# A planned attention and FFN kernel on one core: Sinkhorn of batch 0 ahead, a written-out order, and the last two output projections by Strassen blocks

## The chip, the cores and the metric

The kernel runs on one core of one Trainium2 chip. TensorE multiplies matrices into PSUM, VectorE (DVE), ScalarE (ACT) and GpSimd (POOL) work on what it leaves, and SyncE (SP) and GpSimd issue the transfers between the DRAM and the on-chip SBUF. The metric is the device time of one execution in microseconds (us); less is better. A profiled execution leaves a trace, and a profile page is made from it.

## What is computed

Inputs are q, k and v of shape (4, 8, 768, 64): 4 batches, 8 heads, 768 tokens, 64 wide; `sort_net` (4, 8, 8, 8); and three weight matrices.

```python
P = sort_net                                   # (4, 8, 8, 8)
for _ in range(5):                             # Sinkhorn
    P = exp(P - max(P, axis=-1))
    P = P / (sum(P, axis=-1) + 1e-9)
    P = P / (sum(P, axis=-2) + 1e-9)
k_sorted = einsum('bhij,bhjcd->bhicd', P, k in 8 blocks of 96)
v_sorted = einsum('bhij,bhjcd->bhicd', P, v in 8 blocks of 96)
attn = softmax(q_block @ k_sorted_block.T / 8)  # each block of 96 tokens with its own block only
x = (attn @ v_sorted_block) as (3072, 512)
out = ((x @ w_a) * (x @ w_b)) @ w_out           # 512 -> 1536 -> 512
```

## The kernel before

**Pieces of work and a planner.** The kernel doesn't issue instructions as it goes. It collects pieces of work with `add(engine, duration, function, deps, get, put, rank)` (L49): the engine, or several that could do it, each with an assumed duration; the pieces it depends on; the buffers that it takes and gives back; and a rank. `Plan.solve` (L132) simulates the engines with these durations, with fixed delays between engines (L39) and with a limited number of buffers and PSUM banks. At each step it takes the piece that can start first, and among those that can start within a small margin the one of lowest rank. If a piece may run on two engines, the engine where it would end first is taken. The result, sorted by start, is the order in which `emit` (L992) issues everything; on the chip each engine then works through its own queue in that order. `_fill` (L177) puts warm-up matmuls on zeros into TensorE's planned gaps up to 32.6 us.

**Loads.** GpSimd issues all loads of q, k, v and of the weights, cast to bf16 on the way: k, v and half of q of four head pairs of batch 0, then w_a and w_b in four pieces (`load_ab`, L377) with the other halves of q between the first and the second piece, then batches 1, 2 and later 3. SP issues `sort_net`, the way of v through DRAM (`v_out`, L544; `v_back`, L548), two kinds of transposing transfers and the stores.

**Sinkhorn** (L412 to L453). The 32 matrices of all batches lie one to a partition, 32 x 64. Each of five iterations is an exponential on ScalarE and six VectorE operations, each waiting for the one before. The result is copied out 16 times (`p_rep`), turned by eight small matmuls (`spread_ops`, L432) and multiplied with a mask into `s_all` (`spread`, L439): batch 0 on VectorE, batches 1 to 3 later on GpSimd (`later_spreads`, L455). `s_all` is what k and v are mixed with.

**Attention** goes by head pair (two heads, 128 rows). `mix_half` and `mix_part` mix and transpose k and v with `s_all` on TensorE, `q_part` transposes q, `so_part` (L693) does the scores, the exponential, the product with v and the division, and `x_part` or a transposing transfer puts the result into `xT`. Batch 0 goes in two halves of four blocks each, so that its first half can go on early; later batches go whole, between the other work.

**Up projection.** Batch 0 is done plainly (`ab_plain`, L745): for each of 2 token halves and 12 tiles of the hidden width, four matmuls of 384 columns with w_a, four with w_b; ScalarE copies the first result out (L755), VectorE multiplies the two (L760) into `hT`. Batches 1 to 3 use the Winograd form of Strassen's seven products (`ab_strassen`, L810): the operands are cut into 2 x 2 blocks, seven block products take the place of eight. The sums of weight blocks are made once (`w_sums`, L769, on GpSimd, between the loads); the sums of x per batch (`x_sums`, L789). A chain of products accumulates in one PSUM bank, and between two products of it ScalarE copies out what stands there ("snap", L840); VectorE adds such copies to other banks ("plus", L848). All elementwise operations of two tensors are recorded at L306, the helper `tt`.

**Output projection** (`out_plain`, L893): for each batch, token half and chunk of 128 tokens, 12 matmuls of 512 columns (L899) of `hT` with `w_out_sb` into one bank, of which ten can go before the last tiles of h are there; ScalarE or VectorE copies the bank out, and SP stores it with two transfers (L919).

**Order of the main loop** (L962): the output of batch b, attention of b + 2, loads of b + 3, then the up projection of b + 1.

Of the kernel before, what the change touches and what calls it, by code (L numbers as in the profile page):

```python
# [21 lines left out]
class Op:  # L22
# [3 lines left out]
                 "left", "users", "seq", "ready")  # L26

    def __init__(self, alts, fn, deps, get, put, rank, lat, seq):
        self.alts, self.fn, self.get, self.put = alts, fn, get, put
        self.deps = [d for d in deps if d is not None]  # L30
        self.rank, self.lat, self.seq = rank, lat, seq
        self.start = self.end = self.eng = None
        self.users, self.left, self.ready = [], 0, 0.0


class Plan:
# [12 lines left out]
    def add(self, eng, dur, fn, deps=(), get=(), put=(), rank=0.0, lat=None):  # L49
        alts = dict(eng) if isinstance(eng, (list, tuple)) else {eng: dur}  # L50
        op = Op(alts, fn, deps, list(get), list(put), rank, lat, len(self.ops))
# [80 lines left out]
    def solve(self):  # L132
# [5 lines left out]
        at = dict(self.AT)  # L138
        ready = [op for op in self.ops if op.left == 0]
        done = 0  # L140
        while ready:
            cands = {}
            for op in ready:
# [4 lines left out]
                ends = {e: max(at[e], w) + d for e, d in op.alts.items()}  # L148
                e = min(ends, key=ends.get)
                cands.setdefault(e, []).append((max(at[e], w), op))  # L150
            pick = None
            for e, c in cands.items():
                lo = min(s for s, _ in c) + self.EPS[e]
                s, op = min(((s, o) for s, o in c if s <= lo), key=lambda x: (x[1].rank, x[1].seq))
# [5 lines left out]
            s, e, op = pick  # L160
            ready.remove(op)
            op.start, op.eng, op.end = s, e, s + op.alts[e]
            at[e] = op.end
            self._take(op, s)
# [27 lines left out]
STRASSEN_AB = (1, 2, 3)  # L192
STRASSEN_OUT = ()
# [5 lines left out]
def kernel(  # L199
# [86 lines left out]
    ring("o", 3, [P, DMODEL], FP32)  # L286
# [7 lines left out]
    p_col = const.tile([P, NB, BH], BF16, name="p_col")  # L294
    p_nat = const.tile([BH, NB, NB], FP32, name="p_nat")
    ident = const.tile([P, P], BF16, name="ident")
    mask = const.tile([P, CG], BF16, name="mask")
    rsum = const.tile([BH, NB], FP32, name="rsum")
    csum = const.tile([BH, NB], FP32, name="csum")
    p_fin = const.tile([BH, NB, NB], BF16, name="p_fin")  # L300
    p_rep = const.tile([BH, NB, NB, CG], BF16, name="p_rep")
    warm_sb = const.tile([P, 512], BF16, name="warm_sb")
# [15 lines left out]
    def sp_dma(issue, work, fn, deps, get=(), put=(), rank=0.0):  # L318
        i = add("SP", issue, fn, deps, get=get, rank=rank, lat=0.6)
        return add("DQ", work, None, [i], put=put, rank=rank - 100.0, lat=1.5)  # L320

    o_p = add("SP", 0.1, lambda: nc.sync.dma_start(
        out=p_nat, in_=sort_net.rearrange("b h i j -> (b h) i j")), lat=1.5)
# [739 lines left out]
```

The softmax here doesn't subtract the row's maximum and nothing guards it: scores larger than these inputs give would overflow.

## Time and profile before

| | us |
|---|---|
| median of three runs | 245.91 (245.87 to 340.56) |
| profiled execution | 245.06 |
| its span, first to last instruction | 243.3 |
| TensorE (PE) busy | 233.7 |
| VectorE (DVE) busy | 150.1 |
| ScalarE (ACT) busy | 125.3 |
| GpSimd (POOL) busy, with its issuing of loads | 119.6 |
| output projection, 288 matmuls of 512 columns | 66.4 |
| up projection of batch 0, 192 matmuls of 384 columns | 39.2 |
| warm-up matmuls of 512 columns, 38 | 10.8 |

The granted TensorE clock is 1.0 throughout. A row of a timeline has start, duration, engine, line, operation, what is written and read, and in brackets how long the engine was idle before and what ended that. A row of the chain has start, duration, engine, tensor and line, and "issue" is time in which the engine waited for nothing that the profile shows. A row of a window has its bounds and length, and then the busy time of TensorE, of its weight loads, of VectorE, ScalarE and GpSimd, the clock, the share of the DMA engines and GB/s. A matmul's listed duration overlaps its neighbour's, so the pace of a run of matmuls is its time divided by their number.

### The profile page before, as it was taken

Reading aid. Unit: us, or ns where it says so; the run is one execution under the profiler, and the core shown is the slowest. Engines: PE = TensorE matmul, PEld = TensorE weight load, DVE = VectorE, ACT = ScalarE, POOL = GpSimd, SP = SyncE. Lnnn points to the kernel's source line nnn. Section 1 sums busy time; section 2 is a strip of 40 time slices with the busy share of each in tenths; the row PEclk is TensorE's granted clock in tenths of the full one; section 3 lists DMA queues with packets and bytes.
Section 4 is the critical chain, followed back from the end, with each engine's and each line's share of the span. In section 5 each row is a group of like instructions: output and inputs, shape, how many; then the busy total and the mean of one; then the engine's idle time right before and its main releaser. Section 6 shows DMA issues by size and latency. Waiting matters only on the chain.

```text
span 243.3 us, 5723 instructions
## 1 busy us (share of the span) xinstructions
PE 233.7 (96%) x2204; PEld 132.4 (54%) x2204; DVE 150.1 (62%) x348; ACT 125.3 (52%) x243; POOL 119.6 (49%) x132
## 2 busy tenths in 40 slices
PE   6998999999989999999999999999999999999992
PEld 2466766666655554665544455665654455565440
DVE  6656654654555738589987452988862448886210
ACT  3366646468655533667654443766631076673100
POOL 8979999999970020069755110173540007355000
PEclk9999999999999999999999999999999999999999
DMA  5999999999965683619998867200035450000135
GB/s 67 180 203 187 202 203 187 167 191 178 162 134 107 167 184 78 149 16 154 135 175 110 192 174 178 46 0 0 3 66 108 96 122 0 1 0 3 43 86 129
DMA packets 50106, 27.90 MB, mean 115 GB/s; under 512 B 28832, under 2 KB 47008, under 8 KB 50080
## 3 DMA queue, kind: packets, MB, share of 16 engines
q0 software_dynamic: 24112, 14.16, 43.3%
q1 hardware_dynamic: 25968, 13.38, 25.7%
q8 instruction: 17, 0.28, 0.5%
q14 instruction: 9, 0.07, 0.1%
HBM read 30.29 MB, written 8.26 MB: 158 GB/s over the span
## 4 chain that ended last, share of the span: by engine, by line
PE 67%; ACT 1%; DVE 1%; issue 0%; ACTq 0%; DVEq 0%
PE ps L831 33%; PE ps L899 26%; PE ps L593 2%; PE ps L578 2%; PE ps L489 1%; PE ps L537 1%; PE ps L473 1%; PE ps L749 1%; ACT f L840 0%; DVE xp L604 0%; ACT o L248 0%; DVE a L306 0%; DVE rec L599 0%; ACTq L840 0%; DVEq L306 0%
## 5 line engine op out<-in xcount | busy, mean ns | idle before, releaser
L306 POOL TENSOR_TENSOR hT<-a,f 128x384 bf16<-128x384 bf16 x39 | 35.5, 918 | 78.1 <-DVE f L306 56.3
L899 PE MATMUL ps<-w_out_sb,hT 128*128 128x512 bf16 x288 | 66.4, 379 | 0.0
L840 ACT COPY f<-ps 128x384 f32<-128x384 f32 x108 | 48.2, 482 | 23.6 <-PE ps L831 21.1
L899 PEld LDWEIGHTS <-hT 128*128 128x128 bf16 x288 | 27.0, 98 | 30.1
L306 DVE TENSOR_TENSOR a<-f,ps 128x384 bf16<-128x384 f32 x54 | 29.4, 549 | 10.4 <-PE ps L831 6.4
L306 DVE TENSOR_TENSOR f<-f,ps 128x384 f32<-128x384 f32 x54 | 28.9, 550 | 8.9 <-PE ps L831 6.0
L583 ACT ACTIVATE eT<-ps 96x768 bf16<-96x768 f32 x32 | 24.9, 806 | 17.2 <-PE ps L578 16.9
L306 DVE TENSOR_TENSOR hT<-a,ps 128x384 bf16<-128x384 bf16 x42 | 23.1, 551 | 12.4 <-PE ps L749 6.9
L248 ACT COPY o<-ps 128x512 f32<-128x512 f32 x15 | 8.8, 585 | 36.3 <-PE ps L899 36.3
L831 PE MATMUL ps<-tx,ws_a 128*128 128x384 bf16 x108 | 25.2, 326 | 0.2 <-ACT f L840 0.2
L831 PE MATMUL ps<-tx,ws_b 128*128 128x384 bf16 x108 | 24.9, 326 | 0.3 <-ACT f L840 0.3
L604 DVE TENSOR_TENSOR xp<-ps,rec 96x512 bf16<-96x512 f32 x32 | 21.4, 677 | 0.4
L749 PE MATMUL ps<-xT,w_a_sb 128*128 128x384 bf16 x96 | 19.6, 327 | 0.0
L749 PE MATMUL ps<-xT,w_b_sb 128*128 128x384 bf16 x96 | 19.6, 326 | 0.0
L831 PEld LDWEIGHTS <-ws_b 128*128 128x128 bf16 x144 | 13.8, 98 | 10.1 <-ACT f L840 0.9
L755 ACT CAST a<-ps 128x384 bf16<-128x384 f32 x24 | 11.5, 479 | 14.9 <-PE ps L749 9.1
L250 DVE COPY o<-ps 128x512 f32<-128x512 f32 x9 | 6.2, 691 | 20.8 <-PE ps L899 20.7
L831 PEld LDWEIGHTS <-ws_a 128*128 128x128 bf16 x144 | 13.5, 98 | 10.1 <-ACT f L840 1.4
L831 PE MATMUL ps<-xT,w_b_sb 128*128 128x384 bf16 x72 | 17.6, 326 | 0.3 <-DVE xp L604 0.2
L831 PE MATMUL ps<-xT,w_a_sb 128*128 128x384 bf16 x72 | 17.5, 326 | 0.0
L831 PEld LDWEIGHTS <-w_b_sb 128*128 128x128 bf16 x108 | 10.4, 98 | 7.9 <-DVE xp L604 0.7
L831 PEld LDWEIGHTS <-w_a_sb 128*128 128x128 bf16 x108 | 10.3, 98 | 7.9 <-ACT f L840 0.6
(90 smaller groups left out, 337.9 us busy)
## 6 DMA issues: line engine op xcount, KB each, us to landing
out_dram<-o SPq DMA_DIRECT2D x48, 128.0 KB, 2.4
k<-in_k_dram POOLq DMA_DIRECT2D x16, 192.0 KB, 6.1
v<-in_v_dram POOLq DMA_DIRECT2D x16, 192.0 KB, 6.1
vd<-vm SPq DMA_DIRECT2D x10, 192.0 KB, 2.9
vs<-vd SPq DMA_DIRECT2D x10, 192.0 KB, 3.1
q<-in_q_dram POOLq DMA_DIRECT2D x16, 96.0 KB, 6.9
w_a_sb<-in_moe_w_a_dram POOLq DMA_DIRECT2D x4, 384.0 KB, 7.1
w_b_sb<-in_moe_w_b_dram POOLq DMA_DIRECT2D x4, 384.0 KB, 9.0
```

What stands on the lines that cost most here:

```text
L248: nc.scalar.copy(out=out, in_=in_)
L250: eng.tensor_copy(out=out, in_=in_)
L306: ENG[eng].tensor_tensor(out=out, in0=in0, in1=in1, op=op)
L578: nc.tensor.matmul(sc[:, e, i * BLK:(i + 1) * BLK], lhsT=kT[e * D:(e + 1) * D, at:at + P], rhs=rhs, start=True, stop=True)
L583: nc.scalar.activation(out=buf(("eT", b, p, h))[:, :, 0:HB], in_=buf(("sc", b, p, h))[0:BLK, :, 0:HB], func=AF.Exp, scale=float(scale))
L593: nc.tensor.matmul(ops_[:, e, i * OW:(i + 1) * OW], lhsT=eT[:, e, i * BLK:i * BLK + P], rhs=vs[:, h * NBH + i, e * OW:(e + 1) * OW], start ...
L604: nc.vector.tensor_tensor(out=_ap(xp, h * NBH * 2 * D, [[NB * 2 * D, BLK], [D, 2], [2 * D, NBH], [1, D]]), in0=_ap(ops_, 2, [[1024, BLK], ...
L749: nc.tensor.matmul(pf[:, 0:HW], lhsT=w_sb[:, kc, m * P:(m + 1) * P], rhs=buf(("xT", b))[:, kc, t * HW:(t + 1) * HW], start=(kc == 0), stop ...
L755: ea = add("ACT", 0.48, lambda: nc.scalar.copy(out=buf(("a", b, t, m)), in_=buf(("pf", b, t, m, "a"))[:, 0:HW]), [pa], get=[("a", ("a", b, ...
L831: nc.tensor.matmul(buf(key)[:, 0:HW], lhsT=lf(j), rhs=rf(j), start=start and j == 0, stop=j == 1, skip_group_check=not start)
L840: return add("ACT", 0.48, lambda: nc.scalar.copy(out=buf((name, b, g, n)), in_=buf(kA)[:, 0:HW]), [dep], get=[("f", (name, b, g, n))], rank=r)
L899: nc.tensor.matmul(po, lhsT=hT[:, t * 2 + m // G, m % G, c * P:(c + 1) * P], rhs=w_out_sb[:, m, :], start=(m == 0), stop=(m == KO - 1), sk ...
```

## The change

1. **Sinkhorn.** Batch 0 gets its own, with its 64 rows (8 heads x 8 rows) on 64 partitions. Row sums come from the exponential's accumulator or VectorE's; column sums of a head come from a small f32 matmul with a constant matrix that is one within a head. It ends in one matmul and the same spread. Batches 1 to 3 run the old five iterations on 24 partitions, after batch 0's, with a later rank (12); their copies, matmuls and spreads also come later.
2. **Output projection of batches 2 and 3** by seven block products (`out_strassen`): tokens in two halves, hidden width in two halves, 256 output columns. Per batch 24 sums of `hT` blocks (VectorE or GpSimd) into buffers of k and v that are free by then; once 8 sums of `w_out` (`o_sums`) into buffers of q and kT. Per chunk of 128 tokens seven products of six matmuls of 256 columns, three ScalarE snapshots and four VectorE sums out of PSUM, and two stores of two transfers each.
3. **Planner.** A piece of work can be marked to use the SBUF port that VectorE and GpSimd share (`port`); marked pieces on these engines don't overlap in the plan. The order and, where there is a choice, the engine of every piece are no longer chosen by rank but read from a literal, `ORDER`.
4. **Smaller edits.** The weight pieces load in the order 0, 2, 1, 3. The weight sums of the second piece may run on VectorE too. One more output buffer, and four that lie in `s_all`. The warm-up matmuls read from a part of `ws_b`. The up projection of batch 3 starts after the fifth product of batch 2's last output chunk. Assumed durations: scores 0.33 for 0.23, v's way through DRAM with 3.0 for 1.5 in batch 1.

```diff
+        def begin(op, e, w):
+            return max(at[e], w, port) if e in op.port else max(at[e], w)
...
+        while ready:
+            s, e, op = given() if order else greedy()
...
+            if e in op.port:
+                port = op.end
...
-STRASSEN_OUT = ()
+ORDER = (
...
+STRASSEN_OUT = (2, 3)
+PLAIN_G = 6
...
-    for c in range(1, 4):
+    for c in (2, 1, 3):
         load_ab(c)
...
+    x = step("ACT", 0.28, lambda: nc.scalar.activation(
+        out=pa[:, 1, :], in_=pa[:, 0, :], func=AF.Exp, accum_out=ps1), [o_p0])
+    x = step("DVE", 0.15, lambda: nc.vector.reciprocal(out=pc1, in_=ps1), [x])
+    x = step("DVE", 0.21, lambda: stt(p_exp, _ap(pa, NB, [[2 * NB, HN], [0, H], [1, NB]]), pc1,
+                                      m_same), [x, o_same])
+    x = step("PE", 0.2, sk_turn, [x, o_row], get=[("bank", bank)])
+    x = step("DVE", 0.19, lambda: nc.vector.reduce_sum(
+        out=ps1, in_=buf(bank)[0:HN, 0:NB], axis=AX.X), [x])
+    x = step("DVE", 0.15, lambda: nc.vector.reciprocal(out=pc1, in_=ps1), [x])
+    for it in range(4):
+        x = step("ACT", 0.24, lambda it=it: nc.scalar.activation(
+            out=pa[:, 1, :], in_=px if it else buf(bank)[0:HN, 0:NB], func=AF.Exp, scale=pc1), [x])
+        x = step("PE", 0.2, sk_rows, [x, o_same])
+        x = step("DVE", 0.19, lambda: nc.vector.reciprocal(out=pr, in_=buf(bank)[0:HN, NB:2 * NB]),
+                 [x], put=[bank])
+        x = step("DVE", 0.25, lambda: stt(px, pa[:, 1, :], 1.0, pr, ps1), [x])
+        x = step("DVE", 0.15, lambda: nc.vector.reciprocal(out=pc1, in_=ps1), [x])
...
+    def out_strassen(b, rk, wt_ok):
...
+            todo = ((0, lambda g=g: (hb(1, 0, g), hb(1, 1, g)), ALU.add, h21 + h22, None),
+                    (1, lambda g=g: (sb(0, g), hb(0, 0, g)), ALU.subtract, h11, 0),
+                    (2, lambda g=g: (hb(0, 0, g), hb(1, 0, g)), ALU.subtract, h11 + h21, None),
+                    (3, lambda g=g: (hb(0, 1, g), sb(1, g)), ALU.subtract, h12, 1))
...
+            s1 = snap("os1", p1)
+            p2 = pe(kX, h(0, 1), wo(1, 0), True, True, hd(0, 1, first) + wo_in, rk + 0.1,
+                    get=[("bank", kX)], gs=first)
+            p2 = pe(kX, h(0, 1), wo(1, 0), False, True, hd(0, 1, late) + [p2], rk - 0.4, gs=late)
+            c11 = plus("os1", kX, 0, 0, [s1, p2], [kX, ("os1", b, c)])
+            p6 = pe(kA, s(1), wt(1), False, True, [s1] + sd(1) + td(1), rk, put=sput(1) + tput(1))
+            u2 = snap("ou2", p6)
+            p5 = pe(kY, s(0), wt(0), True, True, sd(0) + td(0), rk + 0.1, get=[("bank", kY)],
+                    put=sput(0) + tput(0))
+            st["lasty", b] = p5
+            p7 = pe(kA, s(2), wt(2), False, True, [u2] + sd(2) + td(2), rk, put=sput(2) + tput(2))
+            u3 = snap("ou3", p7)
+            p4 = pe(kZ, h(1, 1), wt(3), True, True, [p1, p2] + hd(1, 1) + td(3), rk + 0.6,
+                    get=[("bank", kZ)], put=tput(3))
+            c22 = plus("ou3", kY, 1, 1, [u3, p5], [("ou3", b, c)])
+            c21 = plus("ou3", kZ, 1, 0, [u3, p4], [kZ, ("ou3", b, c), ("och", b, c)])
+            p3 = pe(kY, s(3), wo(1, 1), False, True, [c22] + sd(3), rk, put=sput(3))
+            c12 = plus("ou2", kY, 0, 1, [u2, p3], [kY, ("ou2", b, c), ("och", b, c)])
...
     for b in range(B):
-        for t in range(2):
-            for c in range(3):
-                out_plain(b, t, c, RB + 40.0)
+        if b in STRASSEN_OUT:
+            if wt_ok is None:
+                wt_ok = o_sums(RB - 10.0)
+            out_strassen(b, RB + 40.0, wt_ok)
+        else:
+            for t in range(2):
+                for c in range(3):
+                    out_plain(b, t, c, RB + 40.0)
```

## The prediction

> **What bounds the kernel now.** I read the page first: busy shares, then the chain that ended last.
>
> ```profile
> span 243.3 us, 5723 instructions
> PE 233.7 (96%) x2204; PEld 132.4 (54%) x2204; DVE 150.1 (62%) x348; ACT 125.3 (52%) x243; POOL 119.6 (49%) x132
> ...
> PE ps L831 33%; PE ps L899 26%; PE ps L593 2%; PE ps L578 2%; PE ps L489 1%; PE ps L537 1%; PE ps L473 1%; PE ps L749 1%; ACT f L840 0%; DVE xp L604 0%; ACT o L248 0%; DVE a L306 0%; DVE rec L599 0%; ACTq L840 0%; DVEq L306 0%
> ```
>
> TensorE is busy 96% of the span, and the chain is its own queue: the up projections (L831) and the output projection (L899), one matmul after another. So only two things can save time: fewer TensorE microseconds, or fewer microseconds in which it does nothing useful. The chain in order of time shows the second half piece by piece (start, duration, what):
>
> ```profile
> 118.46 0.49 ACT f L840
> ...
> 126.05 0.04 issue
> 126.09 0.49 ACT f L840
> ...
> 151.01 0.19 issue
> 151.20 0.21 DVE rec L599
> 151.42 0.02 issue
> 151.44 0.70 DVE xp L604
> ...
> 238.68 0.02 issue
> 238.70 0.59 ACT o L248
> ```
>
> The breaks are few: 0.56 us at 118.4, 0.6 at 126.0, 1.2 at 151.0, and 1.05 more at 210.8. The last matmul ends at 238.68, and 4.6 us of eviction and store follow.
>
> The start is the other loss. In the timeline:
>
> ```profile
> 2.29 0.26 ACT L414 ACTIVATE p_nat<-p_nat 32x64 f32<-32x64 f32 x1 [0.27 <-DMA p_nat<-in_sort_net_dram]
> ...
> 13.47 0.36 PE L435 MATMUL ps<-ident,p_rep 32*128 32x32 bf16 x8
> ...
> 14.42 0.38 PE L500 MATMUL ps<-s_all,k 128*64 128x64 bf16 x12
> ```
>
> Before 14.42 TensorE has only transposes of q and warm-up matmuls on zeros (L983), which count as busy. The Sinkhorn chain from 2.29 to 13.95 sets this. From the middle of the kernel I take the windows of one stage each (columns: window, length, then busy microseconds by engine): up projection of batch 2, its output projection, up projection of batch 3, and the rest.
>
> ```profile
> 152.00:182.00 30.00, 29.83 (x193) 17.78 (x193) 24.54 (x52) 18.78 (x43) 13.64 (x15) 1.00 0.11 23
> 182.00:195.00 13.00, 13.00 (x63) 5.92 (x61) 4.45 (x8) 1.76 (x3) 0.00 (x0) 1.00 0.47 101
> 195.00:225.00 30.00, 29.90 (x181) 17.34 (x180) 22.16 (x44) 18.91 (x43) 12.73 (x14) 1.00 0.10 23
> ```
>
> TensorE is full; VectorE (third busy number) is at 82% beside an up projection and 34% beside an output projection; GpSimd (fifth) has room.
>
> **Change, part 1: Sinkhorn of batch 0 first, alone, in another layout.** Now one iteration takes 1.76 us (the exponentials start at 2.29, 4.05, 5.81, 7.57, 9.33), then replication until 12.60 (ScalarE's copy waits behind a q copy), a matmul at 13.47 held back by warm-up matmuls, the spread at 13.95. New, from the rows of small instructions: exponential 0.26, reciprocal 0.19, multiply 0.21, TensorE step about 0.2 (one small matmul takes 0.17 to 0.21), 0.12 from TensorE to VectorE (13.83 to 13.95), 0.03 to 0.04 at each other handover. First round: 0.26 + 0.19 + 0.21 + 0.2 + 0.12 + 0.21 + 0.19 + 5 x 0.035 = 1.55. Each of the four others: exponential, TensorE, reciprocal, multiply with sum (0.25), reciprocal: 0.26 + 0.2 + 0.12 + 0.19 + 0.25 + 0.19 + 4 x 0.035 = 1.35, together 5.4. Last multiply, one matmul, handover 0.6. From 2.29 this is 9.85: 4.1 us earlier than 13.95. Below: each of the six TensorE steps stands in a queue with q transposes that wait for loads and with warm-up matmuls; one such delay cost 0.87 here (12.60 to 13.47), so six eat 5.2 and the gain is nothing. Above: the 0.87 of now goes too, 4.4 at most, for what follows is set by loads. Landings (issue plus time to landing): v of pairs 0 to 3 at 7.7, 10.6, 13.1 and 15.5, w_b's first piece at 20.3. The fourth pair's v is mixed at 18.66 now, so it can move by 3.1; w_b's first use is at 28.12, so that is no limit. TensorE, ScalarE and VectorE have other mixes in the meantime. I take 3.6 us, nearer the upper end, since the four loads allow 3.1 and the chain 4.1.
>
> What moves behind: the Sinkhorn of batches 1 to 3, 5 x (0.26 + 1.27) + 0.41 x 2 + 0.42 = 9 us of small work, mostly VectorE's, now has to be done before batch 1 is mixed (48.4 now). VectorE is busy 15.3 of 24 us from 16 to 40, and 5.6 of 10 after: it fits, as long as ready evictions are not queued behind it; if that cover went, up to 9. The three spreads of 2.0 on GpSimd's queue move behind the weight loads; those issued at 17.6 and 20.4 now behind spreads can go earlier, but the transfers are at 200 GB/s from 12 us on, so they land little sooner. The second small load on SP costs one issue (0.41), hidden under the table load (to 2.02). The weight pieces in the order 0, 2, 1, 3 cost nothing: piece 1 lands at 23.7 and 25.7, and TensorE has half 1 of batch 0 until then. Eight sums of w on VectorE (0.55) instead of GpSimd (1.66) free 13 us of GpSimd, which is nobody's limit there (all sums done by 71.4, first needed at 99).
>
> **Part 2: output projection of batches 2 and 3 by seven products.** Removed: 2 x 72 matmuls of 512 columns, 144 x 0.216 (12 in 2.59) = 31.1. Added: 2 x 126 of 256 columns. No row has 256; 384 columns cost 0.1636 (154 in 25.19), so a straight line through 384 and 512 gives 0.111: 252 x 0.111 = 28.0. Gain 3.1. Ends: 0.108 (half of 512) gives 3.9; 0.1636 loses 10.1; it breaks even at 0.123. Each matmul loads its own weights, 98 ns, below 0.111, and rows of 128 columns run eight in 0.45 with weight loads between, so I stay on the line.
>
> The Trainium skill speaks against this step. TensorE: Matmul & The Clock Gate, section Back-to-back issue gap, gives a sustained pace of about 81 ns at 128 columns and 131 ns at 512 when weights are loaded each time; interpolated (an estimate from that page), 252 x 98 ns against 144 x 131 ns would be a loss of 5.8 us. The trace has 216 ns at 512 columns with a weight load each, so the measurement decides.
>
> Added beside it: per batch 24 sums of h (128x384, bf16), 9 ScalarE snapshots, 12 VectorE sums out of PSUM; once 8 sums of w_out; gone: 6 evictions a batch. Prices: a sum of h lies between half of the 768-wide bf16 row (0.55 / 2 = 0.28) and the 384-wide row with an f32 input (0.556); 0.33, nearest to the row of its own type. On GpSimd 0.92. A sum out of PSUM: between 0.55 x 256/384 = 0.37 and 0.55, 0.42. A snapshot 0.38 (0.48 at 384, 0.585 at 512), 18 of them 6.8 on ScalarE, which is at 63% and falls to 14%: hidden. VectorE from 152 to the end: 53.6 + 48 x 0.33 + 24 x 0.42 + 8 x 0.55 - 4 x 0.69 = 81.1 of about 83.6 us of TensorE time. That is too full; with 28 of the sums on GpSimd it is 71.9, or 86%. What does TensorE lose at such a load? From 110 to 130 VectorE is busy 9.08 and 8.78 of 10 us, and TensorE loses 0.25 and 0.29: 2.7%, over 83.6 us 2.3; at 82% (152 to 182) it loses 0.17 in 30. I take 1.3 us; ends 0 and, with all on VectorE and its idle 18% kept, 81.1 / 0.82 - 83.6 = 15.
>
> GpSimd and VectorE clearly meet in one place: a GpSimd sum at 139.12 begins under a VectorE sum and takes 1.83 instead of 1.63 us. So a meeting costs 0.2; fifteen of them 3 us of slack, inside the 15. The Trainium skill (SBUF — State Buffer, section SBUF: two separate sides) is harder: two-input VectorE operations and GpSimd operations exclude each other for the whole instruction. By it, as an estimate, 48 sums that meet GpSimd's share of 31% and wait half of 0.92 lose 6.8 us. No run here shows this.
>
> **Part 3: an order written out for all instructions.** It can take away the breaks at 118.4, 126.0 and 151.0 (2.35) and cannot take more than is there (the break at 210.8 is in the stage just priced). Ends 0 and 2.35; 1.8. If the model behind the order is off, breaks come back elsewhere; that is in the rivals. New waits in it: batch 3's up projection starts behind the fifth product of batch 2's last chunk; now it starts behind its output as well (195.9), so nothing is lost.
>
> **Tail.** The last eviction is 0.42, not 0.59. But a chunk's two stores both come near its end, and SP issues two DMAs in 1.11: one store may stand before the last. The ends are -0.17 and 3.3 (three); net cost 0.3.
>
> **Sum.** 3.6 + 3.1 - 1.3 + 1.8 - 0.3 = 6.9. The profiled execution took 245.06 (span 243.3, 1.76 around it): 238.16. The median of the runs shown, 245.91, is 0.85 above it: 239.0.
>
> **Rivals.** (a) VectorE becomes the bound in the last 84 us. For it: 81.1 of 83.6 us if GpSimd takes none. Against: GpSimd is idle 70% there, and the sums may be made early, during the up projection. With 15 lost rather than 1.3 the time is 252.7: slower. It decides from 8.2 us of loss on (6.9 + 1.3), which is 0.17 for each of the 48 sums.
> (b) The start is hidden anyway: loads, six queued TensorE steps and the displaced Sinkhorn leave 0.5 of 3.6, and the order saves 0.5 rather than 1.8. For it: the fourth pair lands at 15.5, transfers run at 200 GB/s from 12 us on. Against: 18.66 is well behind 15.5. 239.0 + 3.1 + 1.3 = 243.4: within 2%.
> (c) The order does all it could: start 4.4, breaks 2.35, no new loss, no tail: 239.0 - 0.8 - 0.55 - 1.3 - 0.3 = 236.0.
> (d) The smaller matmuls cost 0.123 or more, so the seven products do nothing: 242.1 or more.
>
> **How the numbers follow.** Forecast as worked out, 237.5 to 241.0: 48%. (c), to 234.5 and a little below: 27%. (b) and (d), 241.0 to 246: 17%. (a): 8%, of which most is over 246. 2% of the median is 4.9 us, about what a measurement of this kernel can tell from no change: faster is below 241.0, slower above 250.8. Faster: 48 + 27 + 1 = 0.76; slower 0.06 from (a); the same 0.18. The range takes in (c), (b) and (d) and leaves out (a): 234.5 to 244.0.
>
> **What would show it.** Right: the first mix of k near 10.3 us and the first plain up projection 3 to 4 us before 27.46; out matmuls of 256 columns at 0.108 to 0.112 in runs; VectorE under 92% from the up projection of batch 2 on; last matmul near 232. Wrong: the reciprocal after a small matmul waiting for TensorE by over 0.5 each; TensorE waiting for sums of h or for VectorE's sums out of PSUM by several microseconds; GpSimd's 0.92 grown by VectorE; stores queued at the end. Most of all, the forecast fails if VectorE cannot follow in the two output stages.

## The result, and the profile after

The changed kernel takes 262.15 us (median of four, 259.84 to 262.56), the kernel before 245.89 in the same measurement: a ratio of 1.065, 95% interval 1.057 to 1.073. It is slower, where the forecast was 239.0 and the range ended at 244.0. The profiled execution took 262.37, its span is 260.5. Ratios, here and below, are to the kernel before in the same measurement and leave out executions that are over 1.5% above the fastest of their kernel, while the medians given hold all. The median of the kernel before moved between 245.0 and 245.9 from one measurement to the next, so differences between versions are good to about 1 us.

The page of after, with the lines that answer to those of before, and the granted clock:

```profile
span 260.5 us, 6033 instructions
...
PE 239.5 (92%) x2302; PEld 148.6 (57%) x2314; DVE 181.7 (70%) x429; ACT 129.9 (50%) x261; POOL 129.9 (50%) x149
...
PEclk9995569999999799999999999999999999999998
...
PE 60%; DMA 18%; POOL 10%; DVE 6%; issue 4%; ACT 0%; SPq 0%; DVEq 0%; ACTq 0%
```

TensorE was the chain; now transfers are 18% of it and GpSimd 10%. TensorE is busy 5.8 us longer with less to multiply. In the clock's row, which has forty equal slices of the span, three slices show 0.5 to 0.6 instead of 1.

Where the time goes is seen from the starts of the same pieces in both timelines (the two right columns are versions that come later, z3_five and y6_dve):

| us | before | after | after with four orders put right and warm-ups (z3) | before with the seven products, all sums of xT on VectorE (y6) |
|---|---|---|---|---|
| first mix of k | 14.42 | 14.00 | 12.65 | 14.70 |
| first matmul of batch 0's up projection | 27.46 | 35.23 | 30.45 | 27.90 |
| of batch 1's | 99.03 | 117.89 | 102.97 | 99.01 |
| of batch 2's | 151.53 | 170.29 | 154.22 | 149.79 |
| last matmul ends | 238.68 | 254.90 | 238.80 | 236.58 |
| span | 243.3 | 260.5 | 244.4 | 242.7 |

All of the loss, 18.9 us, is there when batch 1's up projection starts. From the start of batch 2's to the last matmul, the stretch with the seven products, after is shorter: 84.6 us against 87.15. The tail behind it is 5.6 against 4.6.

The start, in TensorE's timeline of after. The first row answers to 13.47 of before, the second to 14.42:

```profile
13.12 0.20 PE L544 MATMUL ps<-p_end,m_rep 64*128 64x64 bf16 x1
...
14.00 0.38 PE L643 MATMUL ps<-s_all,k 128*64 128x64 bf16 x12
...
18.63 0.38 PE L643 MATMUL ps<-s_all,v 128*64 128x64 bf16 x12 [2.12 <-DMA v<-in_v_dram]
...
25.30 0.63 PE L736 MATMUL ps<-vs,eT 96*128 96x66 bf16 x8
26.16 0.27 PE L1284 MATMUL ps<-ws_b 128*128 128x75 bf16 x1 [0.22 <-issue]
26.36 0.53 PE L643 MATMUL ps<-s_all,k 128*64 128x64 bf16 x12
```

The mixes begin 0.42 us earlier, not 4. Then one of them waits 2.12 us for a load of v, and afterwards a group of twelve 64-column matmuls takes 0.53 us where it took 0.38: the clock is down until about 37 us.

The windows, as in the prediction (up projection of batch 2, its output, up projection of batch 3), and the stretch from 80 to 120 us, for after:

```profile
80.00:90.00 10.00, 7.18 (x67) 3.94 (x67) 4.85 (x8) 2.78 (x4) 2.36 (x4) 0.83 1.22 200
90.00:100.00 10.00, 8.29 (x123) 4.52 (x122) 4.56 (x9) 3.83 (x6) 6.13 (x8) 1.00 1.71 171
...
171.00:201.00 30.00, 30.00 (x194) 18.67 (x193) 26.33 (x54) 19.21 (x43) 22.32 (x24) 1.00 0.06 14
201.00:213.00 12.00, 11.66 (x102) 9.53 (x100) 8.88 (x22) 4.45 (x12) 2.77 (x3) 1.00 0.36 70
213.00:243.00 30.00, 29.62 (x195) 18.81 (x194) 26.62 (x54) 17.50 (x40) 22.45 (x25) 1.00 0.22 50
```

TensorE is full in the late stages. From 80 to 120 us it idles 6.8 us (before: 0.25), and the transfers (the last two columns) are heavy. The first two of these windows in before:

```profile
80.00:90.00 10.00, 10.00 (x101) 5.22 (x100) 5.45 (x11) 4.42 (x7) 0.41 (x1) 1.00 0.66 163
90.00:100.00 10.00, 10.00 (x113) 5.62 (x111) 7.04 (x15) 3.34 (x6) 1.23 (x1) 1.00 0.49 118
```

What is TensorE waiting for? In after's waits of that stretch stand a load of k (2.8 us) and v on its way through DRAM, in both directions: 1.6 us for VectorE's copy `vm`, which itself waits for the write before it, and 1.6 us for what comes back. GpSimd's timeline says why. Before:

```profile
106.36 0.92 POOL L306 TENSOR_TENSOR hT<-a,f 128x384 bf16<-128x384 bf16 x1 [1.17 <-DVE f L306]
107.22 0.76 POOL L362 DMA_DIRECT2D k<-in_k_dram  x1
```

After:

```profile
77.81 0.72 POOL L455 DMA_DIRECT2D k<-in_k_dram  x1
85.19 0.72 POOL L455 DMA_DIRECT2D k<-in_k_dram  x1 [6.66 <-PE ps L632]
```

The row at 107.22 in before and the row at 77.81 in after are the same: the first of batch 3's twelve loads. In before it stood behind two products for batch 1's up projection and went out when the ways of v through DRAM were over. In after no such product is ahead of it (those of batch 1 run on VectorE, or behind the loads), so it goes out when the queue reaches it, 29 us earlier, though the plan has it at 99.3; the next waits for a mix of k to free its buffer until 85.19, and most others follow by 96. In the plan (`load_pair`) these loads depend on a division of batch 2's attention. On the chip nothing carries that: the last such division is at 121.00. A transfer beside these loads pays. Landing time of the writes of v to DRAM, from 55 to 125 us, before and after:

```profile
DMA to landing us min/median/max: 1.9/2.8/5.2
```

```profile
DMA to landing us min/median/max: 5.3/7.3/9.8
```

Not all of this is batch 3's doing. The load of k that TensorE waits 2.8 us for is one of batch 2's, issued at 74.25 and landed 9.8 us later, and the first write of v, issued at 74.5, lands in 8.4 us before batch 3's second load goes out. Batch 2's loads are late themselves (the last is issued at 77.10; before, at 65.78), and the next timelines show why.

VectorE and GpSimd in after:

```profile
34.63 3.36 DVE L556 TENSOR_TENSOR p_nat<-p_nat,rsum 24x64 f32<-24x64 f32 x1
```

```profile
34.31 0.74 POOL L455 DMA_DIRECT2D v<-in_v_dram  x1
35.07 1.65 POOL L385 TENSOR_TENSOR ws_a<-ws_a,w_a_sb 128x768 bf16<-128x768 bf16 x1
```

A Sinkhorn product of 24 x 64, 0.21 us otherwise, takes 3.36 beside GpSimd's load issues and weight sum, and another, at 39.02, takes 1.55. The late Sinkhorn reaches `p_col` at 53.4 us instead of 40.5 as planned; GpSimd's spreads wait for it 11.2 us, and batch 1's and 2's remaining loads stand behind the spreads.

### The profile page after: what moved, and what is told of

Its sections match the earlier page's. It is cut to its first block, busy times and chain, and to the rows that moved or that the text cites. A ratio compares the mean times of both kernels' runs of the same rounds, so it can differ in the third digit from the quotient of the medians.

```text
span 260.5 us, 6033 instructions
## 1 busy us (share of the span) xinstructions
PE 239.5 (92%) x2302; PEld 148.6 (57%) x2314; DVE 181.7 (70%) x429; ACT 129.9 (50%) x261; POOL 129.9 (50%) x149
## 4 chain that ended last, share of the span: by engine, by line
PE 60%; DMA 18%; POOL 10%; DVE 6%; issue 4%; ACT 0%; SPq 0%; DVEq 0%; ACTq 0%
PE ps L976 31%; PE ps L1139 9%; DMA vs<-vd 6%; PE ps L1046 5%; DMA vd<-vm 5%; PE ps L893 4%; DMA k<-in_k_dram 4%; DMA v<-in_v_dram 3%; POOL k L455 2%; PE ps L736 2%; PE ps L643 2%; POOL v L455 2%; POOL s_all L581 1%; PE ps L721 1%; DVE p_nat L556 1%
## 5 line engine op out<-in xcount | busy, mean ns | idle before, releaser
L1046 PE MATMUL ps<-w_out_sb,hT 128*128 128x512 bf16 x135 | 32.8, 379 | 0.7 <-issue 0.3
L315 ACT CAST kT<-ps 128x768 bf16<-128x768 f32 (+1 forms) x18 | 12.4, 692 | 16.0 <-PE ps L632 14.1
L1046 PEld LDWEIGHTS <-hT 128*128 128x128 bf16 x144 | 12.7, 98 | 13.1
L736 PE MATMUL ps<-vs,eT 96*128 96x66 bf16 x256 | 13.8, 200 | 3.8 <-DMA vs<-vd 1.9
L899 ACT CAST a<-ps 128x384 bf16<-128x384 f32 x24 | 11.4, 480 | 11.2 <-PE ps L893 8.6
L736 PEld LDWEIGHTS <-eT 96*128 96x128 bf16 x256 | 11.6, 102 | 7.6 <-issue 2.1
L742 DVE RECIPROCAL rec<-ps 96x8 f32<-96x8 f32 x32 | 6.3, 199 | 13.7 <-PE ps L736 13.0
```

Source lines behind the costliest of these rows:

```text
L315: nc.scalar.copy(out=out, in_=in_)
L736: nc.tensor.matmul(ops_[:, e, i * OW:(i + 1) * OW], lhsT=eT[:, e, i * BLK:i * BLK + P], rhs=vs[:, h * NBH + i, e * OW:(e + 1) * OW], start ...
L899: ea = add("ACT", 0.48, lambda: nc.scalar.copy(out=buf(("a", b, t, m)), in_=buf(("pf", b, t, m, "a"))[:, 0:HW]), [pa], get=[("a", ("a", b, ...
L1046: nc.tensor.matmul(po, lhsT=hT[:, t * 2 + m // G, m % G, c * P:(c + 1) * P], rhs=w_out_sb[:, m, :], start=(m == 0), stop=(m == KO - 1), sk ...
```

## The experiments

Theory 1: the loss comes from work that the change displaced in the first 120 us: loads, late Sinkhorn, clock. Theory 2: the seven products cost it, through VectorE and GpSimd. The rest splits these up. Every kernel computes the whole result. Numbers in the edits are those of pieces of work, and "moved" gives them a new place in the order, behind the planner.

### Which part?

**y1_out23**: before, with the seven products alone, order chosen by rank.

```diff
-STRASSEN_OUT = ()
+STRASSEN_OUT = (2, 3)
...
+                op = add((("DVE", 0.33),), None, None,
```

The 24 sums of h per batch are on VectorE only, and the three chunks are staggered in rank.

> The kernel before with one part of the change alone: the output projections of batches 2 and 3 by seven products, order by the ranks as before, the sums on VectorE only, chunks staggered. Theory 1 (all 16 us are lost in the first 120 us, and the seven products are about neutral): 244.5 to 247.5. Theory 2 (VectorE bounds the output stages and that is where the time goes): 250 or more. If the 3.1 us of fewer matmul columns came through: below 243.5.

Measured 249.53; ratio 1.019 (1.013 to 1.025). Between the two theories: the seven products alone cost 4.5 us here. Whether after has the same loss is seen below.

**x2_greedy_noout**: after, without written order and seven products.

```diff
-ORDER = (
...
+ORDER = ()
-STRASSEN_OUT = (2, 3)
+STRASSEN_OUT = ()
```

> The changed kernel without its written-out order (order by the ranks) and without the seven products in the output: new Sinkhorn, load order and port rule stay. Theory 1a (the written-out order is what loses the time): 244 to 250. Theory 1b (the new Sinkhorn and the late Sinkhorn of batches 1 to 3 lose it, in whatever order): 255 or more.

Measured 253.64; 1.031 (1.023 to 1.038): again between the two theories. The Sinkhorn split, with the load order, the port rule and the smaller edits that stay with it, loses about 8 us without the written order. Of what cost after its time, the trace has less: the clock is 0.76 from 20 to 30 us (0.50 in after), and v's writes land in 2.9 us, since its batch 3 loads go out after 110 us. But the late Sinkhorn is late here too: `p_col` comes at 48.1, GpSimd waits 8.5 us for it, and batch 2's last load is issued at 71.2. How the 8 us divide over these was not tested.

### The seven products

In y1's output stage TensorE waits 4.9 us for VectorE (`kT`, a sum of w_out):

```profile
188.17 2.74 PE L994 MATMUL ps<-kT,hT 128*128 128x256 bf16 x12 [4.88 <-DVE kT L306]
```

VectorE's and GpSimd's timelines there:

```profile
178.90 0.63 DVE L306 TENSOR_TENSOR kT<-w_out_sb,q 128x768 bf16<-128x768 bf16 x1
...
182.51 1.99 DVE L306 TENSOR_TENSOR q<-w_out_sb,q 128x768 bf16<-128x768 bf16 x1
...
186.13 1.98 DVE L306 TENSOR_TENSOR kT<-w_out_sb,q 128x768 bf16<-128x768 bf16 x1
```

```profile
182.13 3.86 POOL L306 TENSOR_TENSOR tx<-xT 128x768 bf16<-128x768 bf16 x2
185.96 3.65 POOL L306 TENSOR_TENSOR tx<-xT,tx 128x768 bf16<-128x768 bf16 x2
```

Beside GpSimd's sums of xT, VectorE's sum takes as long as GpSimd's (1.93 each); by itself it takes 0.55 to 0.63. Two experiments take the meeting away.

**y3_apart**: y1, with batch 3's sums of xT after the sums for the seven products, in the plan. The new dependence had no effect on GpSimd's queue, so only the two sums that the plan gave to VectorE moved.

```diff
-            op = add(al, None, None, list(deps) + extra + [home], put=[("xT", b)], rank=rank)
+            op = add(al, None, None, list(deps) + extra + [home, st.get(("S", b - 1))], put=[("xT", b)],
+                     rank=rank)
```

> The kernel before with the seven products in batches 2 and 3 alone (249.5 us when it was run first), and one dependence more: the four differences of batch 3's xT for the up projection, which GpSimd made at 182 to 189.6 us beside VectorE's sums for the seven products, start only when those sums are done. No sum is added or taken away. Port theory: VectorE's 768-column sums beside GpSimd's (1.98 us) go back to 0.6 us, the wait of 4.9 us for kT is gone, and the time is 243.5 to 245.5 us, about that of the kernel before. Rival: there are simply too many sums for VectorE in that stage, or 126 matmuls of 256 columns are no faster than 72 of 512: it stays at 248.5 us or more.

Measured 247.22; 1.008 (1.005 to 1.011). Two meetings less: the wait is 3.4 us, the time 2.3 shorter. Neither of the expected times was met: GpSimd's two other sums still stand at 182.24 to 186.10, beside VectorE's.

**y6_dve**: y1, with all four on VectorE.

```diff
-        al = (("DVE", 0.55), ("POOL", 1.75))
+        al = (("DVE", 0.55),) if b == 3 else (("DVE", 0.55), ("POOL", 1.75))
```

> The kernel before with the seven products in batches 2 and 3 alone, and all four differences of batch 3's xT for the up projection on VectorE. (In the run before this one, two of them were still made by GpSimd at 182.2 to 186.1 us, and VectorE's sums beside them took 1.7 to 2.0 us; TensorE's wait for kT fell from 4.9 to 3.4 us and the time from 249.5 to 247.2.) Port theory: with no GpSimd sum beside them VectorE's 768-column sums take 0.55 to 0.63 us, the wait for kT is under 0.7 us, and the time is 243.8 to 245.3 us, in spite of 2.2 us more work for VectorE. Rival: VectorE has too much to do there in any case: the wait is 2 us or more, and the time 246.5 us or more.

Measured 244.45; 0.9963 (0.9944 to 0.9982): 0.6 us under the kernel before, with more work for VectorE. The rows that answer to 182.51 and to TensorE's wait:

```profile
182.40 0.55 DVE L306 TENSOR_TENSOR q<-w_out_sb,q 128x768 bf16<-128x768 bf16 x1
```

```profile
183.74 1.48 PE L994 MATMUL ps<-kT,hT 128*128 128x256 bf16 x12 [0.56 <-DVE kT L306]
```

Against y1 this is 5.1 us for four sums that changed engine. So y1's loss is the meeting, and not the amount of VectorE's work, which grew.

**y2_out3**: before, with the seven products in batch 3 alone.

```diff
-STRASSEN_OUT = ()
+STRASSEN_OUT = (3,)
```

Unlike y1, it lets GpSimd take sums of h and ranks them earlier.

> The kernel before with the seven products in batch 3's output projection alone, where no next batch's sums are made. The matmuls' part by the traces is 72 times 0.216 less 126 times 0.111, 1.6 us less. Port theory: nothing meets, and what is left is that gain less a longer tail (0.8 us more between the last matmul and the end in the runs with seven products): 244.0 to 245.3 us against 245.0. Rival: the sums ahead of the first product, and the snapshots of partial products, cost TensorE more than the 1.6 us wherever they stand: 246.5 us or more.

Measured 245.33; 0.9999 (0.9976 to 1.0022), at the edge of the first expectation. The 1.6 us of matmuls go to a wait of 1.3 us for the sums of h that come last, and to the tail. In the last stage there is nothing to do meanwhile.

In after itself the meetings are few: from 165 us to the end TensorE waits 1.3 us. So this is not after's loss.

### The start

**x3_v03**: after, with the load of v that was issued behind w_a's first piece ahead of it.

```diff
+        moved = {33: 9.5}
```

> The changed kernel with one transfer moved: the load of v that TensorE waits for from 16.5 to 18.6 is issued ahead of the first piece of w_a instead of behind it. Theory 1c (the halved TensorE clock from 20 to 37 us, brought on by that wait, costs several us): the clock stays at 1.0, the first plain up projection is at 29 or earlier instead of 35.2, the time is 253 to 258. Rival: what follows is set by the loads and the late Sinkhorn, so the gain is taken back by 100 us: 260 to 263.

Measured 258.89; 1.052 (1.044 to 1.059): between the two expectations, 2 to 3 us better than after. The first plain up projection comes at 32.4, not 29: the wait for v is gone, but the clock still falls to 0.5, at 27.4 us and for 6.8 us, after TensorE had been idle 1.8 us in pieces between 20 and 28.

**x4_ws**: after, with GpSimd's eight weight sums behind batch 2's loads.

```diff
+        moved = {498: 68.2, 496: 68.21, 494: 68.22, 495: 68.23, 499: 68.24, 500: 68.25, 501: 68.26, 497: 68.27}
```

> The changed kernel with the eight weight sums on GpSimd moved behind the loads of batch 2 in its queue; nothing else. Theory 1d (VectorE's multiplies of two tensors in SBUF wait for GpSimd's sums, 3.36 and 1.55 us instead of 0.21, so the late Sinkhorn, the spreads and the loads behind them are late): the multiplies take 0.2 to 0.3, the copy of the Sinkhorn result is at 47 or earlier instead of 53.5, the time is 252 to 258. Rival (the multiplies were held by something else, or the late Sinkhorn is late through TensorE and ScalarE anyway): copy after 50, time 260 to 263.

Measured 258.34; its four executions (253.65 to 260.47) scatter too much for a ratio. The median is just above the expected 252 to 258, and no more than 3 to 4 us better than after. The Sinkhorn products are back at 0.21 us:

```profile
39.10 0.21 DVE L559 TENSOR_TENSOR p_nat<-p_nat,rsum 24x64 f32<-24x64 f32 x1
```

But `p_col` still comes only at 51.7, since in this run TensorE waited 3.06 us for v at 18.17 and the clock was down until 40 us.

**c1_warm**: after, with warm-up matmuls in the wait for v.

```diff
+        extra = {op.seq: op.start for op in self.ops if op.seq in (177,)}
+        for t in extra.values():
+            w = Op({"PE": 0.0}, lambda: self.warm_fn(5120), [], [], [], 0.0, None, -1)
+            w.eng, w.start, w.end = "PE", t - 1e-4, t
+            self.ops.append(w)
```

> The changed kernel with ten more warm-up matmuls of 512 columns (2.2 us by the 0.216 us of one) ahead of the mix that waits 2.12 us for the load of v of batch 0's last head pair: the wait stays, but TensorE isn't idle in it. Clock theory: the granted clock stays near 1 from 19.7 to 36.9 us (it was 0.5 there), groups of twelve 64-column matmuls take 0.38 us again (0.53 in the changed kernel), the first plain up projection starts at 30 to 31.5 us (35.2), and the time falls by 3 to 5 us, to 257 to 259 us. Rival: what was lost at the start is waited for again later, at the loads between 80 and 120 us: under 1 us of gain, 261 us or more.

Measured 259.75; 1.056 (1.051 to 1.062). The clock is 1.0 up to 90 us and the first plain up projection starts at 30.80, as expected: 4.4 us earlier. Only about 2 arrive at the end. At batch 1's up projection 2.6 are left (115.28 against 117.89): the rest is waited for between 80 and 100, where v's way through DRAM now costs 5.7 us in one wait. The time lies between the two expectations: the rival was half right.

**c2_half**: c1, with half the columns in the warm-ups between the Sinkhorn steps.

```diff
-            cols = int((o.start - t - 0.06) * rate)
+            cols = int((o.start - t - 0.06) * rate) // (2 if 3.0 < t < 12.0 else 1)
```

> The same ten warm-up matmuls, and the warm-up matmuls between 3 and 12 us, between which the Sinkhorn steps of batch 0 stand in TensorE's queue, cut to half their columns. Theory: these hold up the steps (VectorE waited 5.1 us for them over four steps); with half the columns the first mix of k comes at 12.0 to 13.0 us (14.0 in the changed kernel) and the time falls by a further 0.5 to 1.5 us against the kernel with the ten matmuls alone. Rival one: k, v and q of batch 0 set the start anyway (q's transposes wait for q's loads in the same queue): the first mix stays at 13.6 us or later. Rival two: the shorter bursts let the clock fall: the granted clock is under 0.8 in some stretch before 20 us, and the time is longer by 2 us or more.

Measured 259.34; 1.055 (1.050 to 1.060), the same as c1. The trace is of the longest of the four executions (262.14). In it the first mix comes at 13.67, and groups of twelve take 0.53 us until 17 us, where after's take 0.38 from 9.9 us on: with shorter warm-ups the clock comes up late, near what rival two had, without the loss it named. Not much was won here in this way.

### What TensorE waits for between 80 and 120 us

**x6_loads**: after, with nine load issues ahead of the spreads.

```diff
+        moved = {257: 41.2, 249: 41.202, 276: 41.204, 264: 41.206, 265: 41.208, 285: 41.21, 286: 41.212, 270: 41.214,
...
```

> The changed kernel with one thing moved: nine of GpSimd's issues (five loads of batch 1 and batch 2's q, v and k, one piece of w_out), which stand in its queue behind the spreads of batches 1 to 3, are issued ahead of the first spread. Theory Q: the spreads wait for p_col (11.2 us in the changed kernel), the loads wait behind them, and that is what starves TensorE between 80 and 120 us (6.8 us idle there). Then the load stream goes on at about 200 GB/s between 43 and 53 us, where it was at 41 to 124 GB/s, TensorE is busy for over 37 of the 40 us from 80 to 120 (33.2 in the changed kernel), and the time falls by 4 to 7 us, to 255 to 258 us. Rival: the waits there are the way of v through DRAM and the transfers' own contention, whenever the loads are issued: under 1.5 us of gain, 260.5 us or more.

Measured 263.22; 1.075 (1.070 to 1.080). No gain, as the rival had it; but the time doesn't settle theory Q. The loads did flow (154 and 162 GB/s from 40 to 60 us) and less was lost from 80 to 120 (3.3 us instead of 6.8), but VectorE and GpSimd now met at the weight sums:

```profile
60.99 3.93 DVE L388 TENSOR_TENSOR ws_b<-w_b_sb,ws_b 128x768 bf16<-128x768 bf16 x1
```

TensorE waited 4.1 us for the product behind it, more than was won later.

**x7_three**: x3, x4 and x6 together.

```diff
+        moved = {33: 9.5, 498: 68.2, 496: 68.21, 494: 68.22, 495: 68.23, 499: 68.24, 500: 68.25, 501: 68.26, 497: 68.27,
+                 257: 41.2, 249: 41.202, 276: 41.204, 264: 41.206, 265: 41.208, 285: 41.21, 286: 41.212, 270: 41.214,
...
```

> The changed kernel with three orders put right at once: the load of v that came behind the first piece of w_a is ahead of it, GpSimd's eight sums of up-projection weights come behind batch 2's loads, and the nine issues are ahead of the spreads. If the three causes are separate, their gains add (about 3.3 and 4 us, measured one by one, and 4 to 7 us expected of the third): 248 to 251 us. If they are one cause seen three times (whatever comes first hides the others), the gain is no more than the largest: 254 us or more. It keeps the Sinkhorn split and the seven products in batches 2 and 3, so 248 us would leave the loss that the seven products alone showed (4.5 us).

Measured 255.08; 1.041 (1.035 to 1.046). By the time this is the second expectation, 254 us or more. By the gain it isn't one cause seen three times: 6 to 7 us against after is about the sum of x3 and x4, and more than either. v's writes still land in 5.9 us.

**z1_hold**: after, with batch 3's loads held back: GpSimd first reads from what the last way through DRAM brings.

```diff
+        w = Op({"POOL": 0.0}, self.hold_fn, [], [], [], 0.0, None, -1)
+        w.eng, w.start, w.end = "POOL", 99.31, 99.31
+        self.ops.append(w)
...
+    tiny = const.tile([8, 2], BF16, name="tiny")
+    plan.hold_fn = lambda: nc.gpsimd.tensor_copy(out=tiny, in_=buf(("vs", 2, 3))[0:8, 0, 2:4])
```

> The changed kernel, and GpSimd copies four bytes of each of eight rows of what the last way of v through DRAM brought back (batch 2's last head pair) before it issues batch 3's twelve loads. In the kernel before these loads stand behind GpSimd's products for batch 1's up projection and go out from 107 us on, after the ways through DRAM; in the changed kernel nothing stands ahead of them, and they go out from 85 to 96 us, beside them: the write of v to DRAM lands in 7.3 us there (median from 55 us on), 2.8 in the kernel before. Theory L (the loads of batch 3 come too early): the writes land in 2.5 to 4 us, TensorE's idle time between 80 and 120 us (6.8 us) falls under 3, and the time falls by 3.5 to 6 us, to 256 to 258.5 us. Rival: it is batch 2's loads, late by 10 us, that meet the ways through DRAM: the writes still land in 5 us or more and the time is 260.5 us or more.

Measured 253.88; 1.033 (1.026 to 1.039): about 8 us less than after, more than expected. GpSimd's timeline and two windows:

```profile
104.71 0.18 POOL L1293 COPY tiny<-vs 8x2 bf16<-8x2 bf16 x1 [30.11 <-DMA vs<-vd]
```

```profile
80.00:90.00 10.00, 9.63 (x146) 5.62 (x145) 5.73 (x11) 6.07 (x8) 0.00 (x0) 1.00 1.13 212
90.00:100.00 10.00, 9.94 (x113) 5.44 (x112) 5.65 (x12) 4.17 (x6) 0.00 (x0) 1.00 0.78 160
```

The writes land in 3.8 us (median), and TensorE idles 0.55 us from 80 to 120, though batch 2's last load is issued at 73.87, only 3 us earlier than in after and 8 later than in before. Part of the 8 may be run to run: this execution's clock was down for a shorter time at the start (0.87 and 0.79 from 20 to 40 us, 0.50 and 0.67 in after), and its first plain up projection comes at 32.80, 2.4 us earlier, before the hold can act.

**b_early**: the other way round, the kernel before with batch 3's loads early, and nothing else.

```diff
+        for i in range(589, 613):
+            self.ops[i].start = 87.0 + 0.01 * (i - 589)
```

> The kernel before with one thing moved: batch 3's twelve loads stand in GpSimd's queue behind its sums of up-projection weights (done at 71.4 us), ahead of its difference of xT at 89.6 and its products at 104 and 106 us, and so go out as soon as batch 2's mixes have freed their buffers. No Sinkhorn split, no seven products, no written order. Theory L (these loads beside v's ways through DRAM are what cost the changed kernel most): the writes of v land in 5 to 7 us (2.8 before), TensorE waits 3 to 8 us between 75 and 110 us, and the time is 248.5 to 253.5 us. Rival: with batch 2's loads in time, the ways through DRAM don't suffer: landings under 4 us, 246.5 us or less.

Measured 256.29; 1.045 (1.038 to 1.051): 11 us lost, more than expected. The row of GpSimd that answers to 107.22 of before, TensorE's timeline at the worst place, and the writes:

```profile
71.44 0.74 POOL L364 DMA_DIRECT2D k<-in_k_dram  x1
```

```profile
89.17 1.04 PE L595 MATMUL ps<-vs,eT 96*128 96x66 bf16 x16 [6.03 <-DMA vs<-vd]
```

```profile
DMA to landing us min/median/max: 2.2/6.6/10.9
```

Twelve loads whose issue begins at 71.4 instead of 107.2 us do to the old kernel what the change did. TensorE idles 8.4 us from 80 to 120, its clock is 0.5 for 6.8 us behind the longest wait, and batch 1's up projection starts at 110.0 instead of 99.0. Theory L is shown from both sides; what it costs in after is known less well, 6 to 8 us (z1, and z2 below).

### Do the causes add up?

**z2_four**: x7 and z1 together.

```diff
+        moved = {33: 9.5, 498: 68.2, 496: 68.21, 494: 68.22, 495: 68.23, 499: 68.24, 500: 68.25, 501: 68.26, 497: 68.27,
...
+        w = Op({"POOL": 0.0}, self.hold_fn, [], [], [], 0.0, None, -1)
```

> The kernel with three orders put right (255.1 us: the load of v ahead of w_a, GpSimd's weight sums behind batch 2's loads, nine loads ahead of the spreads), and batch 3's loads held behind the last way of v through DRAM. Theory L: a further 2.5 to 5 us, 250 to 252.5 us, with landings of 2.5 to 4 us; what is left against 245 is then the half clock between 20 and 36 us. Rival: under 1.5 us, 253.6 us or more, since batch 2's loads and the ways meet anyhow.

Measured 249.38; 1.013 (1.006 to 1.020), a little better than expected: 5.7 us less than x7.

**z3_five**: z2, and four and six warm-up matmuls ahead of the two groups that waited for a load in x7 (pieces 177 and 188).

```diff
+        extra = [(op.start, {177: 4, 188: 6}[op.seq]) for op in self.ops if op.seq in (177, 188)]
+        for t, n in extra:
+            w = Op({"PE": 0.0}, lambda n=n: self.warm_fn(512 * n), [], [], [], 0.0, None, -1)
```

> The kernel with four orders put right, and four and six warm-up matmuls of 512 columns ahead of the two matmul groups that waited for a load there (0.76 us for v at 16.4 and 1.32 us for q at 21.3 us in the kernel with three), so that TensorE isn't idle. Clock theory: the granted clock stays at 1 from 20 to 36 us, the first plain up projection starts at 28.5 to 30.5 us (33.05 with three orders), and since nothing after it is late any more, most of it stays: 2 to 4 us less than with four, 247 to 250 us. Rival: it is waited for again later: less than 1 us of gain.

Measured 246.16; 1.004 (1.001 to 1.007), a little better than expected. The clock is 1.0 throughout. All parts of the change are in it. It is 1.0 us above the kernel before, where after was 16.3 above: about 15 of the 16 us were places in a queue, and the clock that fell in the waits they caused. By the table, what z3 still loses by batch 1's up projection (3.9 us) and in the tail (1.0) is won again behind it (1.25 in batch 1's stage, 2.6 in the last).

## Why the prediction was wrong

- **Part 3, the written order: "Ends 0 and 2.35".** This is the step that failed first of all. I priced the order only by breaks on TensorE and set its worst at zero. An order fixes places in a queue, not times: what held batch 3's loads back in before were two products in GpSimd's queue, and the order left none ahead of them. Undone in after that is 6 to 8 us; done alone in before it costs 11. With three more places put right and warm-up matmuls in two waits, it is about 15 us (z3), for a term that I had at 1.8 of gain. "If the model behind the order is off, breaks come back elsewhere; that is in the rivals" named it in general, but no rival had its place or price. Following GpSimd's queue past every moved load would have shown it: at 104.27 and 106.36 the products stand there, before 107.22.
- **Part 1, the start: 3.6.** Wrong too: without the order and the seven products this part, with the smaller edits, loses about 8 us (x2). Four of the six TensorE steps held VectorE up for 5.1 us (waits for L513, 2.0 the longest), behind warm-ups and transposes. That is the lower end I gave ("six eat 5.2 and the gain is nothing"), and I took a value near the upper. The first mix came 0.42 us earlier, and the load of v of the fourth pair, now issued behind w_a's first piece, made TensorE idle 2.12 us and its clock fall. Keeping the clock up alone gives 4.4 us at 35 us (c1).
- **Part 1, "it fits, as long as ready evictions are not queued behind it".** It did not fit: beside GpSimd's weight sums the late Sinkhorn's products grew from 0.21 to 3.36, `p_col` came at 53.4, the spreads and the loads behind them late. x3, x4 and x6 together, the load of v included, give 6 to 7 us.
- **Part 2, 3.1 less 1.3 for VectorE.** About right in after: the stretch from batch 2's up projection to the last matmul is 2.5 us shorter (1.8 forecast), with 1.3 us of waits. The pace of 256 columns is 0.110 (48 matmuls from 188.38 to 193.66 in y6), 0.111 forecast.
- **"So a meeting costs 0.2".** Wrong for a VectorE sum with both inputs in SBUF: 1.4 (1.99 less 0.55). The changed kernel's plan keeps such sums apart (`port`), and after itself loses little in the last stages; y1, without that plan, loses 4.9 us in one wait. That is not rival (a), VectorE as the bound: y6 gives VectorE more work and has none of y1's loss. The Trainium skill's rule (SBUF — State Buffer, section SBUF: two separate sides: for a VectorE operation with two inputs in SBUF the shared pair of ports is locked for a whole instruction) agrees with 1.99 beside GpSimd's 1.93, where I had written that no run shows it.
- **Tail, 0.3.** It lost 1.0. At the end one store waits behind the other for SP, as feared: VectorE's last sum ends at 255.36, its store is issued from 256.48 on.

Rival (b), a start that is hidden anyway, was nearest in mechanism, and at 243.4 still 19 us off. Rival (a) was nearest in time, 252.7, by a mechanism that after doesn't show: VectorE is busy 26.62 of 30 us at most in the windows above, and TensorE's waits from 165 us on are 1.3 us. None of the cases had transfers that come too early.

## What to carry to other kernels

A planned time holds nothing back on the chip; only what stands ahead in the same queue, or a semaphore, does. So for each transfer that an edit moves, or whose neighbours in the queue move, ask what held it before and what it would run beside if it went at once. Keep GpSimd's sums away from VectorE's where both read only SBUF, or give them all to VectorE, even at more work for it. A wait of 1 or 2 us early on may cost several more through the clock; warm-up matmuls in it are cheap.

## What the runs showed of the hardware

- What meets depends on the operands: VectorE's sums with both inputs in SBUF grow beside GpSimd (0.55 to 1.99, 0.21 to 3.36, 0.55 to 3.93), while those with one input from PSUM stay at 0.54 beside GpSimd's products (y1, 179 to 181 us). It goes both ways: GpSimd's product at 179.08, begun under VectorE's sum at 178.90, took 1.24 for 0.92.
- After 2.12 us of idle TensorE the granted clock is 0.5 for some 17 us (after); ten warm-up matmuls in the same wait keep it at 1.0 (c1). In before, an idle microsecond between 18 and 20 us had no such effect, while in x3 1.8 us in pieces were followed by 6.8 us at 0.5; where the limit lies is not shown. The Trainium skill (TensorE: Matmul & The Clock Gate, section Part 1: The HAM clock gate) says that the clock is halved unless recent activity releases it, which agrees as far as the halving goes.
- v's write of 192 KB to DRAM lands in 2.8 us where the transfer engines' share is 0.49 to 0.66 (before, 80 to 100 us), and in 6.6 to 7.3 beside the loads, where it is 1.2 to 1.7 (after, b_early). v takes the way twice, with SP's queue between, and TensorE waits 6 us in one place.
